# A short convolution of 464 tokens moved from TensorE to GpSimd, in a kernel of convolution and gated feed-forward layers

## The chip, the cores and the metric

The kernel runs on one core of a Trainium2 chip. The core has TensorE (PE in the profile; its weight loads are PEld), VectorE (DVE), ScalarE (ACT), GpSimd (POOL) and SyncE (SP), which here only issues DMAs. The metric is device time in microseconds; less is better. The median of three runs of the kernel before is 763.82 us (762.99 to 764.46).

## What is computed

The input `x` is 8 x 4096 x 192. Each of the 192 channels belongs to one of 8 heads of 24 channels, and each head has 7 taps, the softmax of its row of `weight`. A causal convolution along the 4096 tokens applies them, and a feed-forward layer of width 1536 with a gate follows:

```python
x_pad = np.concatenate([np.zeros((B, K - 1, D)), x], axis=1)
x_unf = x_pad[:, idx, :].reshape(B, S, K, H, group)      # idx[s, k] = s + k
x = np.einsum('hk,bskhg->bshg', softmax(weight), x_unf)  # the convolution
out = (np.maximum(x @ w_gate, 0) * (x @ w_val)) @ w_out  # the feed-forward layer
```

## The kernel before

**Units.** The 8 sequences are split into two streams of four, which lie side by side on the partitions: 64 channels of stream 0 and 64 of stream 1, in three chunks `c`. A unit is 1024 tokens of both streams, in two windows of 512. There are 16 units. `xc[u]` holds the convolved tokens of unit `u`, channels on partitions.

**Stages of a unit.** `gate_val` (L560 the matmuls, L571 the relu on ScalarE, L572 the product on VectorE) makes 24 blocks of the hidden layer, 12 for each window. The projection (`project_turn`, L582) then runs over three output tiles `p`, each in two turns, in the order (0,0) (1,0) (0,1) (2,0) (1,1) (2,1). After turn 0 of a tile ScalarE copies one column of it (`between_turns`, L595), so that turn 1, which writes the same tile, waits for ScalarE. After turn 1 VectorE transposes the tile into the output buffer (`turn_out`, L600). All PSUM tiles come from one ring of four, `ps`.

**The convolution, two ways.** Units 0 and 1 are convolved on TensorE, with the taps spread into band matrices. Unit 0 by `conv_steps`, straight into `xc[0]`. Unit 1 by `conv(2)` and `conv(3)` (L409), during the projection of unit 0: eight matmuls each, tokens on partitions, then five ScalarE copies out of PSUM (L422) and five DMA transposes into `xc[1]` (L441). `conv(2)` makes the first 560 tokens of unit 1, `conv(3)` the other 464.

Units 2 to 15 are convolved tap by tap off TensorE, by a lane that runs one to two units ahead. For unit `u`: `lane_load` loads the tokens (L250, issued by GpSimd); `lane_turn` lets GpSimd sort them (L462) and the SP queue transpose them (L464) into `x_r`, with the last 16 tokens of the unit before copied in front (L452). During the projection of unit `u-2`, `lane_first` (L510) and `product` (L490) on ScalarE multiply by taps, and `lane_rest` on VectorE runs twelve `scalar_tensor_tensor` steps (L521) and one `tensor_scalar` (L531), in portions of 6, 5 and 2, each ahead of one `turn_out`. During the gate stage of unit `u-1`, GpSimd adds the seven products of the remaining 1792 elements of each partition (`add`, L499), the last add writing `xc[u]`.

**What sets the order.** Nothing is rescheduled (`tc.manual_schedule()`): each engine and each DMA queue runs its instructions in the order in which the program writes them, and waits by semaphores. Most pools have one buffer for a name: `x_e`, `x_p` and each `prod` tile are used again by the next unit, which waits until the last reader is done.

Of the kernel before, what the change touches and what calls it, by code (L numbers as in the profile page):

```python
# [8 lines left out]
FP = mybir.dt.float32  # L9
F16 = mybir.dt.float16  # L10
ACTF = mybir.ActivationFunctionType
ALU = mybir.AluOpType
# [3 lines left out]
def kernel(  # L16
# [12 lines left out]
    nc = tc.nc  # L29

    B, S, D = x.shape
# [4 lines left out]
    NB = B // 2  # L36
# [9 lines left out]
    WARM = [(4, 4, 4, 1), (4, 4, 1)]  # L46
    STEPS0 = [1, 0, 2, 3, 4]
    CONV1 = 10


    UNIT = 2 * WIN
# [4 lines left out]
    TILES = UNIT // 128  # L56
    GROUPS = [(0, [WIN * w + SUB * j for j in range(GSUB)]) for w in range(2)]
    second = [min(t, 2 * UNIT - SUB) for t in range(UNIT, 2 * UNIT, SUB)]
    GROUPS += [(0, second[:GSUB]), (0, second[GSUB:])]

    ctx.enter_context(tc.manual_schedule())
    const = ctx.enter_context(tc.tile_pool(name="const", bufs=1))
# [13 lines left out]
    def staged(i, j):  # L76
        return stages[i][:, XH * j : XH * (j + 1)]
# [163 lines left out]
    def lane_load(u, streams=range(2)):  # L241


        bp, t0 = u * UNIT // S, u * UNIT % S
        if u not in xes:
            xes[u] = epool.tile([128, TILES, 2, NCH, 64], F16, name="x_e"), None
        xe, head = xes[u]
        for st in streams:
            row = (bp + NB * st) * S + t0
            nc.gpsimd.dma_start(  # L250
                out=xe[:, :, st, :, :].rearrange("p j c r -> p j (c r)"),
                in_=bass.AP(
                    tensor=x.tensor,
                    offset=x.offset + row * D,
                    ap=[[D, 128], [128 * D, TILES], [1, D]],
                ),
            )
        if 1 in streams and t0 and u - 1 not in xes and u - 1 not in xrs:
            head = const.tile([HALO, 2, NCH, 64], F16, name="head")
            nc.gpsimd.dma_start(  # L260
                out=head[:].rearrange("p s c r -> p s (c r)"),
                in_=bass.AP(
                    tensor=x.tensor,
                    offset=x.offset + (bp * S + t0 - HALO) * D,
                    ap=[[D, HALO], [NB * S * D, 2], [1, D]],
                ),
            )
        xes[u] = xe, head

    for s in range(4):  # L270
        load_w(s)
# [4 lines left out]
    load_x(1, range(1, 2))  # L276
    for s in (6, 7):
        pool_halves(s)
    lane_load(2, range(1))
    for s in (8, 9):  # L280
        pool_halves(s)
    lane_load(2, range(1, 2))

    mx = const.tile([128, 1], FP)
    nc.vector.tensor_reduce(
# [113 lines left out]
    def conv(g):  # L399


        xt = xts.pop(g)
        bp, toks = GROUPS[g]
        n = len(toks)
        rows = SUB + PAD
        W = 2 * n * G
        pair = [psum.tile([128, 2, 512], FP, name="ps") for _ in range(2)]
        for h, (t, bank, slot) in PLACE.items():
            nc.tensor.matmul(  # L409
                out=pair[t][0:SUB, bank, W * slot : W * (slot + 1)],  # L410
                lhsT=band(h),
                rhs=xt[0:rows, 0:n, :, G * h : G * (h + 1)],
                start=True,
                stop=True,
                skip_group_check=True,
            )
        y = staged(1, g - 1).rearrange("p (j c s r) -> p j c s r", c=NCH, s=2, r=64)
# [28 lines left out]
    def lane_turn(u):  # L446
        xe, head = xes.pop(u)
        xr = rpool.tile([128, NCH, HALO + UNIT], F16, name="x_r")
        if u * UNIT % S == 0:
            nc.gpsimd.memset(xr[:, :, 0:HALO], 0.0)  # L450
        elif head is None:
            nc.gpsimd.tensor_copy(out=xr[:, :, 0:HALO], in_=xrs[u - 1][:, :, UNIT : UNIT + HALO])  # L452
        else:
            turned = const.tile([HALO, NCH, 2, 64], F16, name="turned")
            for st in range(2):
                nc.gpsimd.tensor_copy(out=turned[:, :, st, :], in_=head[:, st, :, :])
            nc.sync.dma_start_transpose(
                out=xr[:, :, 0:HALO], in_=turned[:].rearrange("p c s r -> p (c s r)")
            )
        xp = epool.tile([128, TILES, NCH, 2, 64], F16, name="x_p")  # L460
        for st in range(2):
            nc.gpsimd.tensor_copy(out=xp[:, :, :, st, :], in_=xe[:, :, st, :, :])  # L462
        for j in range(TILES):
            nc.sync.dma_start_transpose(  # L464
                out=xr[:, :, HALO + 128 * j : HALO + 128 * j + 128],
                in_=xp[:, j].rearrange("p c s r -> p (c s r)"),
            )
        xrs[u] = xr

    def pieces(lo, hi):  # L470

# [11 lines left out]
    def flat(u):  # L483
        return xc[u][:].rearrange("p c t -> p (c t)")
# [9 lines left out]
                    scale=tap[:, c, k : k + 1],  # L494
                )

    def add(u, k):
        p0 = prods[u, 0]
        nc.gpsimd.tensor_tensor(  # L499
            out=p0[:] if k < KW - 1 else flat(u)[:, LDVE:FLAT],  # L500
            in0=p0[:],
            in1=prods.pop((u, k))[:],
            op=ALU.add,
        )
# [35 lines left out]
    def gate_val(u, w):  # L540
        h = hpool.tile([128, NFF, 2, WIN], F16, name="hT")
        xcb = xc[u]
        for f in range(NFF):
# [25 lines left out]
            for sts in [slice(0, 1), slice(1, 2)] if u == 0 and w == 0 and f == 0 else [slice(0, 2)]:  # L569
                gr = gpool.tile([128, 2, WIN], F16, name="gr")  # L570
                nc.scalar.activation(out=gr[:, sts], in_=pss[0][:, sts], func=ACTF.Relu)  # L571
                nc.vector.tensor_tensor(out=h[:, f, sts], in0=gr[:, sts], in1=pss[1][:, sts], op=ALU.mult)  # L572
        return h

    def project_turn(hs, p, ps, turn):
# [84 lines left out]
    )  # L660
    for u in range(NUNIT):
        lane = 1 <= u < NUNIT - 1
        if lane:
            add(u + 1, 1)
        if u == 1:
            lane_load(3)
            add(2, 2)
            add(2, 3)
        if u + 2 < NUNIT:
            lane_turn(u + 2)  # L670
        if u == 0:
            xts[3] = load_x(3)
            wide = plain.rearrange("k (f a p d) -> k f a p d", a=2, p=3, d=32)
            for a in range(2):
                nc.gpsimd.tensor_copy(out=Wo[:, :, :, 32 * a : 32 * a + 32], in_=wide[:, :, a, :, :])
        if lane:
            for k in range(4 if u == 1 else 2, KW - 1):
                if k == KW - 2 and 1 < u < NUNIT - 3:
                    lane_load(u + 3, range(1))
                add(u + 1, k)  # L680
            if 1 < u < NUNIT - 3:
                lane_load(u + 3, range(1, 2))
        hs = [gate_val(u, w) for w in range(2)]
        if lane:
            add(u + 1, KW - 1)
        if u == 1:
            lane_load(4)
        if u == 0:
            xc[1] = xcpool.tile([128, NCH, UNIT], F16, name="xc")
            conv(2)  # L690
        del xc[u]
        bp, w0 = u * UNIT // S, u * UNIT % S // WIN
        lane = None
# [9 lines left out]
        for p, turn in ((0, 0), (1, 0), (0, 1), (2, 0), (1, 1), (2, 1)):  # L703
            if turn == 0:
                tiles[p] = psum.tile([128, 2, 512], FP, name="ps")
            project_turn(hs, p, tiles[p], turn)
            if turn == 0:
                between_turns(tiles[p])
                if u == 0 and p == 0:
                    conv(3)  # L710
                if lane:
                    for k in TAPS[p]:
                        product(u + 2, k)
                if u == 0 and p == 1:
                    psum.tile([128, 2, 512], FP, name="ps")
                continue
            if lane:
                for _ in range(STEPS[p]):
                    next(lane)
            turn_out(tiles[p], o, p)  # L720
# [31 lines left out]
```

## Time and profile before

| | |
|---|---|
| median of 3 runs | 763.82 us |
| the profiled execution, its own time | 763.18 us |
| its span | 761.2 us |
| mean granted clock of TensorE | 0.999 |
| busy: PE / DVE / ACT / POOL | 757.1 / 669.9 / 604.0 / 425.0 us |
| start of unit 1, 2, 3 on TensorE | 58.30 / 104.97 / 151.60 us |

The span is what the profiler saw of the engines; the execution's own time has some 2 us more around it. Times on the axis of the trace count from the span's start. In a row of the timeline, the first number is the start, the second how long the instructions of the row lasted from first start to last end, and brackets at the end give the idle time of that engine before it and what ended it. In a group, the numbers behind the bar are the total busy time, the mean of one instruction in ns, and the idle time before them.

### The profile page before, as it was taken

The page shows a single profiled execution, that of the slowest core. Times are in us where ns is not written, and L with a number is a line of the kernel's source. Part 1 is how long each engine was busy: PE and PEld are TensorE (multiplying, and loading weights), DVE is VectorE, ACT ScalarE, POOL GpSimd, SP SyncE. Part 2 cuts the span into 40 slices and gives each one's busy share as a digit, 9 for nine tenths or more (in the row PEclk, how much of TensorE's full clock was granted, in tenths as well). Part 3 has the DMA queues.
Part 4 walks back from the last instruction along what each step waited for, and adds up shares of the span by engine and source line. Part 5 has one row for each costly group of instructions (what it writes and reads, how often), then busy time and mean ns, then how long its engine had stood idle before and what let it go on. Part 6 is the DMA issues. An engine that isn't in the chain of part 4 may idle for free.

```text
span 761.2 us, 30408 instructions
## 1 busy us (share of the span) xinstructions
PE 757.1 (99%) x13732; PEld 497.5 (65%) x13732; DVE 669.9 (88%) x634; ACT 604.0 (79%) x671; POOL 425.0 (56%) x200
## 2 busy tenths in 40 slices
PE   9999999999999999999999999999999999999998
PEld 5556666666666666666666666666666666666668
DVE  7879989998998989989899899998999989896691
ACT  7898887878878788787877878788797887874471
POOL 8608749094591936829277391864909558092000
PEclk9999999999999999999999999999999999999999
DMA  9927536054450534516255152442715432030302
GB/s 149 154 56 131 85 82 86 5 121 49 95 76 6 126 42 98 72 27 119 28 106 65 48 102 23 111 59 70 88 14 121 49 88 42 3 84 3 86 3 84
DMA packets 154513, 54.36 MB, mean 71 GB/s; under 512 B 149632, under 2 KB 154384, under 8 KB 154384
## 3 DMA queue, kind: packets, MB, share of 16 engines
q1 hardware_dynamic: 117600, 37.87, 22.6%
q0 software_dynamic: 36352, 14.26, 17.1%
q8 instruction: 107, 1.75, 0.9%
q10 hardware_dynamic: 432, 0.30, 0.1%
q14 instruction: 22, 0.18, 0.1%
HBM read 29.40 MB, written 25.17 MB: 72 GB/s over the span
## 4 chain that ended last, share of the span: by engine, by line
PE 99%; DMA 0%; ACT 0%; issue 0%
PE ps L560 65%; PE ps L582 31%; PE ps L625 2%; PE ps L386 0%; PE ps L409 0%; DMA w<-in_weight_dram 0%; PE ps L195 0%; PE ps L330 0%; PE ps L211 0%; PE ps L205 0%; ACT out_s L636 0%; ACT L129 0%
## 5 line engine op out<-in xcount | busy, mean ns | idle before, releaser
L572 DVE TENSOR_TENSOR hT<-gr,ps 128x1024 f16<-128x1024 f16 (+1 forms) x385 | 468.9, 1218 | 35.3 <-ACT gr L571 8.3
L571 ACT ACTIVATE gr<-ps 128x1024 f16<-128x1024 f32 (+1 forms) x385 | 392.8, 1021 | 116.5 <-PE ps L560 116.5
L499 POOL TENSOR_TENSOR prod<-prod,prod 128x1792 f32<-128x1792 f32 x70 | 279.5, 3993 | 258.6 <-DVE prod L531 230.8
L560 PE MATMUL ps<-xc,Wg 64*64 64x512 f16 (+1 forms) x4464 | 324.3, 376 | 0.0
L560 PE MATMUL ps<-xc,Wv 64*64 64x512 f16 (+1 forms) x4464 | 324.2, 376 | 0.0
L582 PE MATMUL ps<-hT,Wo 64*64 64x512 f16 x4320 | 236.3, 376 | 0.0
L560 PEld LDWEIGHTS <-Wg 64*64 64x64 f16 (+1 forms) x4464 | 163.5, 107 | 85.2
L560 PEld LDWEIGHTS <-Wv 64*64 64x64 f16 (+1 forms) x4464 | 157.0, 106 | 91.4 <-DVE hT L572 0.3
L582 PEld LDWEIGHTS <-Wo 64*64 64x64 f16 x4320 | 153.9, 107 | 78.9 <-issue 0.3
L490 ACT ACTIVATE prod<-x_r,tap 128x1024 f32<-128x1024 f16 (+1 forms) x182 | 175.1, 1044 | 0.0
L521 DVE SCALAR_TENSOR_TENSOR acc<-x_r,tap,acc 128x1024 f32<-128x1024 f16 (+1 forms) x140 | 113.2, 874 | 2.0 <-ACT acc L510 2.0
L600 DVE STREAM_TRANSPOSE out_s<-ps 128x1024 f32<-128x1024 f32 x45 | 56.1, 1247 | 33.3 <-PE ps L582 28.8
L499 POOL TENSOR_TENSOR xc<-prod,prod 128x1792 f16<-128x1792 f32 x14 | 56.0, 4001 | 0.4
L462 POOL COPY x_p<-x_e 128x1536 f16<-128x1536 f16 x28 | 40.3, 1463 | 0.1
L250 POOL DMA_DIRECT2D x_e<-in_x_dram x28 | 25.5, 911 | 0.0
L595 ACT COPY turned_by<-ps 128x2 f32<-128x2 f32 x45 | 7.0, 156 | 21.8 <-PE ps L582 19.9
L521 DVE SCALAR_TENSOR_TENSOR xc<-x_r,tap,acc 128x1024 f16<-128x1024 f16 (+1 forms) x28 | 24.1, 859 | 0.0
L510 ACT ACTIVATE acc<-x_r,tap 128x1024 f32<-128x1024 f16 (+1 forms) x28 | 21.6, 821 | 0.0
L625 PEld LDWEIGHTS <-hT 128*128 128x128 f16 x192 | 15.8, 98 | 0.4 <-issue 0.4
L625 PE MATMUL ps<-Wo,hT 128*128 128x192 f16 x192 | 16.0, 246 | 0.0
L636 ACT COPY out_s<-ps 128x768 f32<-128x768 f32 (+2 forms) x5 | 3.2, 638 | 12.7 <-PE ps L625 12.7
L636 DVE COPY out_s<-ps 128x192 f32<-128x192 f32 x1 | 0.4, 356 | 13.3 <-PE ps L625 13.3
(58 smaller groups left out, 72.4 us busy)
## 6 DMA issues: line engine op xcount, KB each, us to landing
out_dram<-out_s SPq DMA_DIRECT2D x121, 192.0 KB
x_e<-in_x_dram POOLq DMA_DIRECT2D x28, 384.0 KB, 5.3
x_r<-x_p SPq DMA_TRANSPOSE x112
out_dram<-out_s SPq DMA_DIRECT2D x3, 384.0 KB
out_s<-in_x_dram POOLq DMA_DIRECT2D x4, 240.0 KB, 6.7
prod<-in_moe_w_out_dram POOLq DMA_DIRECT2D x1, 576.0 KB, 9.1
prod<-in_x_dram SPq DMA_DIRECT2D x2, 192.0 KB
out_s<-in_x_dram POOLq DMA_DIRECT2D x2, 192.0 KB, 4.9
```

The lines of the kernel that those rows point to most:

```text
L250: nc.gpsimd.dma_start(out=xe[:, :, st, :, :].rearrange("p j c r -> p j (c r)"), in_=bass.AP(tensor=x.tensor, offset=x.offset + row * D, ap ...
L462: nc.gpsimd.tensor_copy(out=xp[:, :, :, st, :], in_=xe[:, :, st, :, :])
L490: nc.scalar.activation(out=prods[u, k][:, at - LDVE : at - LDVE + n], in_=shifted(u, c, k, t, n), func=ACTF.Copy, scale=tap[:, c, k : k + 1],)
L499: nc.gpsimd.tensor_tensor(out=p0[:] if k < KW - 1 else flat(u)[:, LDVE:FLAT], in0=p0[:], in1=prods.pop((u, k))[:], op=ALU.add,)
L510: nc.scalar.activation(out=accs[u][:, at : at + n], in_=shifted(u, c, 0, t, n), func=ACTF.Copy, scale=tap[:, c, 0:1],)
L521: nc.vector.scalar_tensor_tensor(out=(flat(u) if k == KW - 1 else acc)[:, at : at + n], in0=shifted(u, c, k, t, n), scalar=tap[:, c, k : k ...
L560: nc.tensor.matmul(out=pss[i][q : q + M, st, :], lhsT=W[64 * st : 64 * st + 64, c, 128 * f + q : 128 * f + q + M], rhs=xcb[64 * st : 64 * ...
L571: nc.scalar.activation(out=gr[:, sts], in_=pss[0][:, sts], func=ACTF.Relu)
L572: nc.vector.tensor_tensor(out=h[:, f, sts], in0=gr[:, sts], in1=pss[1][:, sts], op=ALU.mult)
L582: nc.tensor.matmul(out=ps[64 * st : 64 * st + 64, b, :], lhsT=Wo[64 * r : 64 * r + 64, f, p, :], rhs=hs[b][64 * r : 64 * r + 64, f, st, :] ...
L600: nc.vector.transpose(out=o[:].rearrange("p t (b d) -> p b t d", b=2)[:, :, :, 32 * p : 32 * p + 32], in_=ps[:].rearrange("p b (t c) -> p ...
L625: nc.tensor.matmul(out=ps[:, i // 2, D * (i % 2) : D * (i % 2) + D], lhsT=h[:, f, st, 128 * q : 128 * (q + 1)], rhs=Wo[:, f, :, :].rearran ...
```

## The change

`conv(3)` is taken out: its loads, its eight matmuls, its copies and transposes, and a spare PSUM tile allocated beside it. The 464 tokens of unit 1 are convolved tap by tap instead.

- `rest_load` loads the last 512 tokens of unit 1, one DMA for each stream, ahead of the loads of unit 2. `rest_turn` sorts them on GpSimd (two copies of 768 elements) and transposes them (four DMA transposes on SP's queue, in front of the eight of unit 2) into `x_r1`. The 16 tokens in front of unit 2 are now copied from `x_r1`, and the small load `head` and its transpose go.
- `rest_pool`: GpSimd multiplies 3 x 464 elements by taps 0 to 4, the tap broadcast along the tokens, and sums them: five multiplies and four adds. They stand in its queue during unit 0, behind `lane_turn(2)` and the copies of `Wo`. The first product goes into `out_s` space (`rest["sum"]`), the others into a tile of the name `x_p` (`rest["new"]`), which unit 2's transposes read before.
- `rest_scalar`: ScalarE makes the product of tap 6 for two chunks, behind the eighth and the twelfth relu of the second window of unit 0. `rest_vector`: VectorE makes four products, tap 5 for three chunks and tap 6 for one, between the gate stage and the projection of unit 0.
- `rest_end`: at the head of unit 1's instructions GpSimd adds tap 5 (one add of 1392 elements) and tap 6 (three adds of 464), which write the last 464 columns of `xc[1]`.
- In unit 1, GpSimd's order is now: `rest_end`, `lane_load(3)`, adds of unit 2 for taps 6 and 5, `lane_turn(3)`, adds for taps 4, 3, 2, 1, `lane_load(4)`. Before it was: one add, `lane_load(3)`, two adds, `lane_turn(3)`, three adds, `lane_load(4)`. Later units keep their order.

```diff
-    GROUPS += [(0, second[:GSUB]), (0, second[GSUB:])]
+    GROUPS += [(0, second[:GSUB])]
+    REST = SUB * GSUB - WIN
+    NREST = WIN - REST
...
+    xr1 = const.tile([128, NCH, WIN], F16, name="x_r1")
+    def rest_turn():
+        for st in range(2):
+            nc.gpsimd.tensor_copy(out=xp1[:, :, :, st, :], in_=xe1[:, :, st, :, :])
+        for j in range(WIN // 128):
+            nc.sync.dma_start_transpose(
+                out=xr1[:, :, 128 * j : 128 * j + 128],
+                in_=xp1[:, j].rearrange("p c s r -> p (c s r)"),
+            )
...
-    lane_load(2, range(1))
+    rest_load(0)
     for s in (8, 9):
         pool_halves(s)
-    lane_load(2, range(1, 2))
+    rest_load(1)
+    lane_load(2)
...
+    def rest_at(k, cs=slice(0, NCH)):
+        o = REST - KW + 1 + k
+        return xr1[:, cs, o : o + NREST]
...
+    def rest_pool():
+        for k in range(KW - 2):
+            nc.gpsimd.tensor_tensor(
+                out=rest["new" if k else "sum"],
+                in0=rest_at(k),
+                in1=tap[:, :, k : k + 1].to_broadcast([128, NCH, NREST]),
+                op=ALU.mult,
+            )
+            if k:
+                nc.gpsimd.tensor_tensor(
+                    out=rest["sum"], in0=rest["sum"], in1=rest["new"], op=ALU.add
+                )
...
+    def rest_end():
+        nc.gpsimd.tensor_tensor(out=rest["sum"], in0=rest["sum"], in1=rest[KW - 2], op=ALU.add)
+        for c in range(NCH):
+            nc.gpsimd.tensor_tensor(
+                out=xc[1][:, c, WIN + REST : UNIT],
+                in0=rest["sum"][:, c, :],
+                in1=rest[KW - 1][:, c, :],
+                op=ALU.add,
+            )
...
+            if u == 0 and w == 1 and f in RESTF:
+                rest_scalar(RESTF.index(f))
...
         if u == 0:
-            xts[3] = load_x(3)
+            rest_turn()
+            lane_turn(2)
             wide = plain.rearrange("k (f a p d) -> k f a p d", a=2, p=3, d=32)
             for a in range(2):
                 nc.gpsimd.tensor_copy(out=Wo[:, :, :, 32 * a : 32 * a + 32], in_=wide[:, :, a, :, :])
+            rest_parts()
+            rest_pool()
+        elif u == 1:
+            rest_end()
+            lane_load(3)
+            for k in range(KW - 1, 0, -1):
+                if k == KW - 3:
+                    lane_turn(3)
+                add(2, k, 1)
+            lane_load(4)
...
             conv(2)
+            for k, c in [(KW - 2, c) for c in range(NCH)] + [(KW - 1, NCH - 1)]:
+                rest_vector(k, c)
...
-                if u == 0 and p == 0:
-                    conv(3)
...
-                if u == 0 and p == 1:
-                    psum.tile([128, 2, 512], FP, name="ps")
```

More of the change, by code (lines that the diff above doesn't have):

```diff
@@ L48 @@
     CONV1 = 10
+    RESTF = [7, 11]
     UNIT = 2 * WIN
@@ L245, in lane_load @@
         if u not in xes:
-            xes[u] = epool.tile([128, TILES, 2, NCH, 64], F16, name="x_e"), None
-        xe, head = xes[u]
+            xes[u] = epool.tile([128, TILES, 2, NCH, 64], F16, name="x_e")
+        xe = xes[u]
         for st in streams:
@@ L257, in lane_load, with rest_load @@
             )
[L258 to L266, printed above, removed]
+    xe1 = stages[1][:, 0 : WIN // 128 * 2 * D].rearrange("p (j s c r) -> p j s c r", s=2, c=NCH, r=64)
+    xp1 = stages[1][:, XH : XH + WIN // 128 * 2 * D].rearrange(
+        "p (j c s r) -> p j c s r", c=NCH, s=2, r=64
+    )
+    xr1 = const.tile([128, NCH, WIN], F16, name="x_r1")
+    def rest_load(st):
+        nc.gpsimd.dma_start(
+            out=xe1[:, :, st, :, :].rearrange("p j c r -> p j (c r)"),
+            in_=bass.AP(
+                tensor=x.tensor,
+                offset=x.offset + (NB * st * S + UNIT + WIN) * D,
+                ap=[[D, 128], [128 * D, WIN // 128], [1, D]],
+            ),
+        )
[6 more added lines that the diff above has]
+                in_=xp1[:, j].rearrange("p c s r -> p (c s r)"),
             )
-        xes[u] = xe, head
     for s in range(4):
@@ L416, in conv @@
             )
-        y = staged(1, g - 1).rearrange("p (j c s r) -> p j c s r", c=NCH, s=2, r=64)
+        y = staged(1, 0).rearrange("p (j c s r) -> p j c s r", c=NCH, s=2, r=64)
         def move(copy, t, bank, i0, step_in, c, r0, step_out, width):
@@ L446, in lane_turn @@
     def lane_turn(u):
-        xe, head = xes.pop(u)
+        xe = xes.pop(u)
         xr = rpool.tile([128, NCH, HALO + UNIT], F16, name="x_r")
@@ L450, in lane_turn @@
             nc.gpsimd.memset(xr[:, :, 0:HALO], 0.0)
-        elif head is None:
+        elif u > 2:
             nc.gpsimd.tensor_copy(out=xr[:, :, 0:HALO], in_=xrs[u - 1][:, :, UNIT : UNIT + HALO])
[L453 to L459, printed above, removed]
         xp = epool.tile([128, TILES, NCH, 2, 64], F16, name="x_p")
@@ L467, in lane_turn, with rest_parts, rest_scalar, rest_vector @@
             )
+        if u == 2:
+            nc.gpsimd.tensor_copy(out=xr[:, :, 0:HALO], in_=xr1[:, :, WIN - HALO : WIN])
         xrs[u] = xr
+    def rest_at(k, cs=slice(0, NCH)):
+        o = REST - KW + 1 + k
+        return xr1[:, cs, o : o + NREST]
+    rest = {}
+    def rest_parts():
+        rest["sum"] = stages[1][:].bitcast(FP)[:, XH // 2 : XH // 2 + NCH * NREST]
+        held_e = epool.tile([128, TILES, 2, NCH, 64], F16, name="x_e")
+        rest[KW - 1] = held_e[:].rearrange("p j s c r -> p (j s c r)").bitcast(FP)[:, 0 : NCH * NREST]
+        held_p = epool.tile([128, TILES, NCH, 2, 64], F16, name="x_p")
+        rest["new"] = held_p[:].rearrange("p j c s r -> p (j c s r)").bitcast(FP)[:, 0 : NCH * NREST]
+        rest[KW - 2] = xc[0][:].rearrange("p c t -> p (c t)").bitcast(FP)[:, 0 : NCH * NREST]
+        for k in list(rest):
+            rest[k] = rest[k].rearrange("p (c t) -> p c t", t=NREST)
+    def rest_pool():
[10 more added lines that the diff above has]
+                )
+    def rest_scalar(c):
+        nc.scalar.activation(
+            out=rest[KW - 1][:, c, :],
+            in_=rest_at(KW - 1, c),
+            func=ACTF.Copy,
+            scale=tap[:, c, KW - 1 : KW],
+        )
+    def rest_vector(k, c):
+        nc.vector.tensor_scalar(
+            out=rest[k][:, c, :],
+            in0=rest_at(k, c),
+            scalar1=tap[:, c, k : k + 1],
+            scalar2=None,
+            op0=ALU.mult,
+        )
+    def rest_end():
[6 more added lines that the diff above has]
+                op=ALU.add,
+            )
     def pieces(lo, hi):
@@ L495, in product, with add @@
                 )
-    def add(u, k):
+    def add(u, k, last=KW - 1):
         p0 = prods[u, 0]
         nc.gpsimd.tensor_tensor(
-            out=p0[:] if k < KW - 1 else flat(u)[:, LDVE:FLAT],
+            out=p0[:] if k != last else flat(u)[:, LDVE:FLAT],
             in0=p0[:],
@@ L662 @@
         lane = 1 <= u < NUNIT - 1
[L663 to L670, printed above, removed]
         if u == 0:
-            xts[3] = load_x(3)
+            rest_turn()
+            lane_turn(2)
             wide = plain.rearrange("k (f a p d) -> k f a p d", a=2, p=3, d=32)
@@ L675 @@
                 nc.gpsimd.tensor_copy(out=Wo[:, :, :, 32 * a : 32 * a + 32], in_=wide[:, :, a, :, :])
-        if lane:
-            for k in range(4 if u == 1 else 2, KW - 1):
-                if k == KW - 2 and 1 < u < NUNIT - 3:
+            rest_parts()
[8 more added lines that the diff above has]
+            lane_load(4)
+        elif lane:
+            add(u + 1, 1)
+            if u + 2 < NUNIT:
+                lane_turn(u + 2)
+            for k in range(2, KW - 1):
+                if k == KW - 2 and u < NUNIT - 3:
                     lane_load(u + 3, range(1))
                 add(u + 1, k)
-            if 1 < u < NUNIT - 3:
+            if u < NUNIT - 3:
                 lane_load(u + 3, range(1, 2))
         hs = [gate_val(u, w) for w in range(2)]
-        if lane:
+        if lane and u > 1:
             add(u + 1, KW - 1)
-        if u == 1:
-            lane_load(4)
         if u == 0:
```

## The prediction

> **What bounds the kernel now.** I read the page's busy times first, then its chain of waits, then that chain in order of time, to see what the removed piece occupies.
>
> ```profile
> PE 757.1 (99%) x13732; PEld 497.5 (65%) x13732; DVE 669.9 (88%) x634; ACT 604.0 (79%) x671; POOL 425.0 (56%) x200
> PE 99%; DMA 0%; ACT 0%; issue 0%
> ...
> 40.56 0.99 PE ps L409 x8
> 41.55 2.71 PE ps L582 x48
> 44.27 0.96 PE ps L409 x8
> 45.22 13.07 PE ps L582 x240
> 58.30 31.13 PE ps L560 x576
> 89.43 15.54 PE ps L582 x288
> ```
>
> TensorE is the whole chain: whatever it no longer does is saved, and whatever it must wait for is lost, for no later stage has slack to give it back (every unit is 31.1 + 15.54 us of TensorE). The second row of L409 is the piece that goes: 0.96 us. GpSimd is busy 56%, so it looks free; where, its timeline and the table of windows tell (the windows are two projections, a gate stage, a projection).
>
> ```profile
> 31.76 2.23 POOL L675 COPY Wo<-prod 128x1152 f16<-128x1152 f16 x2
> 59.26 4.00 POOL L499 TENSOR_TENSOR prod<-prod,prod 128x1792 f32<-128x1792 f32 x1 [25.27 <-ACT prod L490]
> 63.20 1.81 POOL L250 DMA_DIRECT2D x_e<-in_x_dram  x2
> 65.02 8.08 POOL L499 TENSOR_TENSOR prod<-prod,prod 128x1792 f32<-128x1792 f32 x2
> 73.04 0.24 POOL L452 COPY x_r<-x_r 128x48 f16<-128x48 f16 x1
> 73.19 3.04 POOL L462 COPY x_p<-x_e 128x1536 f16<-128x1536 f16 x2
> ...
> 41.50:58.10 16.60, 16.60 (x297) 9.14 (x300) 13.05 (x16) 16.38 (x28) 0.00 (x0) 1.00 0.24 54
> 89.40:105.00 15.60, 15.60 (x296) 10.42 (x289) 14.07 (x17) 14.51 (x19) 0.65 (x1) 1.00 0.46 53
> 105.00:136.00 31.00, 31.00 (x580) 20.29 (x576) 28.90 (x24) 24.07 (x24) 28.53 (x11) 1.00 0.63 105
> 136.00:151.60 15.60, 15.60 (x296) 10.42 (x290) 14.08 (x17) 14.53 (x19) 0.00 (x0) 1.00 0.01 2
> ```
>
> The hole is 34.0 to 59.3. But the windows (columns PE, PEld, DVE, ACT, POOL) show that GpSimd computes only in gate stages and never in a projection, while VectorE runs its L521 steps (`scalar_tensor_tensor`, two tensors from SBUF) only in projections. No row shows the two side by side. Last, the queue of DMA transposes, ScalarE and VectorE, because the new work hangs on them:
>
> ```profile
> 29.23 11.17 SPq L464 DMA_TRANSPOSE x_r<-x_p  x8
> 76.26 11.61 SPq L464 DMA_TRANSPOSE x_r<-x_p  x8
> ...
> 89.75 1.54 ACT L510 ACTIVATE acc<-x_r,tap 128x1024 f32<-128x1024 f16 x2
> 92.07 0.16 ACT L595 COPY turned_by<-ps 128x2 f32<-128x2 f32 x1 [0.79 <-PE ps L582]
> ...
> 44.22 4.86 DVE L521 SCALAR_TENSOR_TENSOR acc<-x_r,tap,acc 128x1024 f32<-128x1024 f16 x6 [2.00 <-ACT acc L510]
> ```
>
> Eight transposes take 11.2 to 12.3 us. Those of unit 3 end at 87.87 and L510, which reads them, starts at 89.75: under 2 us to spare. Behind L510 in ScalarE's order stands L595, and turn 1 of a projection tile writes over what L595 reads, so TensorE waits for it.
>
> **Removed from TensorE.** `conv(3)`: 0.96 us in the chain. The whole projection of unit 0 is 2.71 + 0.96 + 13.07 = 16.74 against 15.54 in later units, so 0.96 to 1.20; I take 1.1. Its five ScalarE copies (2.00) and five transposes go too, off the path. Unit 1 would start at 58.3 - 1.1 = 57.2. That is the most the change can gain: 0.15%. About 0.2% (1.5 us) is what a measurement of this kernel can tell from no change.
>
> **ScalarE and VectorE products.** Two ScalarE products of 464: L510 takes 1.19 for 1024 and 0.49 for 256, so about 0.7 each. The first stands between two relus that leave 0.27 idle each, so some 0.4 is pushed on; VectorE, at 1.22 of every 1.295, can't recover it; TensorE loses up to 0.4, I take 0.3. The second delays L510 of unit 2, covered by VectorE's 1.55 us idle before its first L600. Four VectorE products (768 elements take 0.61, so some 0.45 each, 1.8 together) fit the 2.00 idle before L521. Path: +0.3.
>
> **When GpSimd can start.** The issues of `load_x(3)` (2.6) and `head` (0.5) go, two loads of 0.76 come; the loads of unit 2 are issued some 3 us later, still before GpSimd needs them at 26. On SP's queue four new transposes stand in front of unit 2's eight: 26.4 + 12 x 1.31 + 0.8 (one of the early ones took 2.05) = 42.9, and the last one lands 1.1 later, as before's did: 44.0. `conv(2)`'s five transposes behind them end near 50, in time for 57. The first multiply needs only the four new ones, but the second writes into the x_p tile that the eight still read (`rest["new"]`). So it starts at 44.0, not in the hole.
>
> **How long.** GpSimd has no two-input row but L499: 1792 elements in 3.99, 4.04 from start to start. Its copies take 0.50 for 384 and 1.46 for 1536, so 0.18 fixed; then 1392 elements are 3.14 and 464 are 1.17. A multiply by a broadcast tap is in no row: between a one-input copy (1392: 1.34) and an add (3.14); I take the add, as both read two operands. From 44.0 there are 4 multiplies, 5 adds and 3 short adds: 9 x 3.14 + 3 x 1.17 = 31.8. `rest_end` ends at 75.8 if nothing disturbs it; TensorE wants its last channel at 57.2 + 15.5 + 0.4 = 73.2, so it stalls 2.6.
>
> **What is moved behind it.** Load, adds and turn of unit 3 come after `rest_end`: load 1.8, two adds 8.1, halo and copies 3.2: 88.9 (before: 76.2). Transposes 11.6 and landing 1.1: 101.6, L510 and L595 1.7: 103.3. TensorE wants turn 1 of the first tile two runs of 2.59 after its projection starts (57.2 + 31.1 + 2.6 = 90.9), at 96.1: 7.2 lost. VectorE's L521 steps start 10 us late (102.6 against 92.5); 1.4 of that is its idle time before L600 and 7.2 is TensorE's own wait, so unit 2's first product is about 1.3 late. Together 2.6 + 7.2 + 1.3 = 11.1 without any interference. Adds of unit 2 end near 105, before unit 2 starts; later units keep their order.
>
> **Interference, the unknown term.** From 44.0 GpSimd's steps lie beside VectorE's twelve L521 steps. The price lies between nothing and full turn-taking. GpSimd takes 2.13 ns an element for two inputs and 0.83 for one, so its adds are bound by reading; rows beside L572 (one tensor from SBUF, one from PSUM) show 3.99 to 4.04, no price, but that is not the form here. I take turn-taking: eleven pairs, GpSimd 9 x 3.14 + 2 x 1.17 = 30.6 and VectorE 4.86 + 3.23 + 1.28 = 9.4, then the last transposes and steps as in the row from 102.83 to 106.34, 3.5. VectorE's first product of unit 1 starts at 44.0 + 43.5 = 87.5 instead of 60.1 - 1.1 + 0.3 = 59.3, and TensorE, which needs the PSUM tiles that VectorE empties, loses 28.2 less the 0.3 it can run ahead. The stalls of the last two paragraphs then vanish, for `rest_end` ends near 85 and unit 1's second half starts only near 101, its projection near 116, after unit 3's transposes (about 110).
>
> The Trainium skill (SBUF — State Buffer, Who interferes with whom) says that a VectorE instruction with two SBUF inputs and a GpSimd instruction that reads SBUF shut each other out for a whole instruction. No row here shows it. By that rule the sum is this one, without it the first rival's.
>
> **Sum.** -1.1 + 0.3 + 27.9 = +27.1 on the profiled execution's 763.18 (span 761.2 and 1.98 around it) is 790.3; the median of the runs is 0.64 above that execution, so 790.9. Pairs are not always both ready, so I say 790.
>
> **Rivals.**
> 1. No interference: GpSimd and VectorE run side by side. For: every add in the page costs the same, whatever VectorE does. Against: never beside L521. +11.1 - 0.8 = 774.1. With multiplies at 2.2 us `rest_end` is 3.8 earlier, the 2.6 goes and the 7.2 is 6.0: 770.
> 2. They exclude each other, but VectorE keeps going while its next step is ready, so GpSimd gets in only between VectorE's runs. First run held 2.9, the later ones by one GpSimd step each: unit 1's first product 5.7 late; `rest_end` ends at 86, 7.0 after it is wanted; then the 7.2 and 1.3 as above and 1 for adds beside L521: 22.2 - 0.8 = 785.2. If GpSimd keeps going instead, VectorE's steps wait for all of it: 44.0 + 31.8 + 9.4 + 1.2 + 3.5 = 89.9 for the first product, 30.6 late, 793.
> 3. Not slower: multiplies at copy speed, no interference and transposes done by 41.5. Then `rest_end` ends at 41.5 + 4 x 1.34 + 5 x 3.14 + 3.5 = 66.1, unit 3's transposes land at 91.9, and L595 is done at 93.6, just when TensorE wants it. It decides at that 66: each us later costs one. Time 763.0. Against: no two-input row near copy speed, and all three must hold.
>
> **Chances.** Forecast 0.43; rival 1 0.27; rival 2 0.18, its variant 0.07; rival 3 0.05, which by its gain of 0.8 is mostly within 0.2%. The range runs from rival 1 with cheaper multiplies (770) to the variant (794); the forecast's own is 786 to 793. Slower 0.95, same 0.03, faster 0.02.
>
> **What would show it.** Right: L521 steps after 44 start 3 us apart, each at the end of a GpSimd step; VectorE's first L572 of unit 1 near 87; a hole of over 20 us in TensorE at the start of unit 1. Rival 1: L521 keeps 1.27, a hole of 2 to 3 us at the middle of unit 1, and one of 7 us before its third projection run, ended by L595. The step on the second multiply is wrong if it starts before 42. The whole is wrong if `rest_end` ends before 67.

## The result: 789.5 us, and the profile after

The changed kernel takes 789.48 us (median of 6 runs, 788.72 to 791.26), the kernel before, run on the same chip, 763.63 (762.85 to 764.46). The ratio is 1.0343, 95% interval 1.0328 to 1.0358: slower by 26 us. The profiled execution took 790.11, its span is 788.4, 27.2 more than before. In the changed kernel the familiar lines have new numbers: gate and value matmuls L633, relu L644, product L645, projection L657, VectorE's convolution steps L594, its transposes of output tiles L675, `between_turns` L670, GpSimd's adds for later units L572. The new work is L505 (multiplies), L512 (adds), L517 (ScalarE's products), L525 (VectorE's products), L534 and L536 (`rest_end`).

First the page, its busy times and its chain, and under it pieces of that chain in order of time (start, duration, what):

```profile
PE 761.6 (97%) x13724; PEld 498.5 (63%) x13724; DVE 695.2 (88%) x638; ACT 603.3 (77%) x668; POOL 459.3 (58%) x211
PEclk9996799999999999999999999999999999999999
PE 89%; DVE 4%; DMA 3%; POOL 2%; issue 1%; SPq 0%; ACT 0%; DVEq 0%; ACTq 0%; POOLq 0%
```

```profile
30.69 7.95 DMA x_r<-out_s
39.33 1.01 ACT gr L644
...
47.79 6.00 DVE xc L525 x2
53.80 3.29 DVE x_e L525
57.08 13.51 DVE acc L594 x5
...
85.56 30.90 PE ps L633 x519
116.46 15.54 PE ps L657 x277
132.00 31.09 PE ps L633 x571
```

TensorE was the whole chain before; now a stretch of the chain ahead of 85.56 is a DMA, then VectorE. From there on a unit again takes 30.9 and 15.54. Unit 1's projection begins at 116.46 (before: 89.43) and unit 2 at 132.00 (104.97): both 27.03 later. So all of the loss is made before unit 1's gate stage is under way, and none is given back. What TensorE waited for (total, times, longest), and GpSimd's and VectorE's timelines in that stretch:

```profile
PE ps L633 <- DVE out_s L675: 20.2, 3, 14.7
PE ps L633 <- ACT gr L644: 2.2, 1, 2.2
```

```profile
41.05 2.51 POOL L505 TENSOR_TENSOR out_s<-x_r,tap 128x1392 f32<-128x1392 f16 x1
45.11 2.51 POOL L505 TENSOR_TENSOR x_p<-x_r,tap 128x1392 f32<-128x1392 f16 x1 [1.55 <-DMA x_r<-x_p]
47.69 3.21 POOL L512 TENSOR_TENSOR out_s<-out_s,x_p 128x1392 f32<-128x1392 f32 x1
...
56.90 2.55 POOL L505 TENSOR_TENSOR x_p<-x_r,tap 128x1392 f32<-128x1392 f16 x1
59.53 4.01 POOL L512 TENSOR_TENSOR out_s<-out_s,x_p 128x1392 f32<-128x1392 f32 x1
...
73.58 4.45 POOL L536 TENSOR_TENSOR xc<-out_s,x_e 128x464 f16<-128x464 f32 x3
```

```profile
46.62 7.18 DVE L525 TENSOR_SCALAR xc<-x_r,tap 128x464 f32<-128x464 f16 x3
53.72 3.37 DVE L525 TENSOR_SCALAR x_e<-x_r,tap 128x464 f32<-128x464 f16 x1
57.01 3.53 DVE L594 SCALAR_TENSOR_TENSOR acc<-x_r,tap,acc 128x1024 f32<-128x1024 f16 x1
...
57.01 18.88 DVE L594 SCALAR_TENSOR_TENSOR acc<-x_r,tap,acc 128x1024 f32<-128x1024 f16 x6
75.80 1.24 DVE L675 STREAM_TRANSPOSE out_s<-ps 128x1024 f32<-128x1024 f32 x1
76.97 4.13 DVE L594 SCALAR_TENSOR_TENSOR acc<-x_r,tap,acc 128x1024 f32<-128x1024 f16 x4
81.02 1.27 DVE L594 SCALAR_TENSOR_TENSOR xc<-x_r,tap,acc 128x1024 f16<-128x1024 f16 x1
...
85.44 1.18 DVE L645 TENSOR_TENSOR hT<-gr,ps 128x1024 f16<-128x1024 f16 x1
```

Six L594 steps take 18.88 us where the same six took 4.86. Read the first of them (the row with x1, from a narrower window) against GpSimd: it starts at 57.01, GpSimd's multiply runs from 56.90 to 59.45, and the step ends at 60.54, 1.09 after that; GpSimd's add starts at 59.53 and ends at 63.54, 3.00 after the step has ended. Each waits inside its own duration, for the whole of the other's instruction. Such a wait shows as a long instruction and not as idle time: the busy share of VectorE is 88% as before, and only its sum has grown by 25.3 us. The four new L525 products are 10.5 of the growth, and L594's group is 15.0 of it (before: 113.2 in all, 874 ns for one):

```profile
L594 DVE SCALAR_TENSOR_TENSOR acc<-x_r,tap,acc 128x1024 f32<-128x1024 f16 (+1 forms) x140 | 128.2, 982 | 0.0
```

The L594 steps that start after GpSimd's last add (78.03) are as short as before. Unit 1's first product is at 85.44 instead of 60.12, 25.3 later. The other 1.7 of the 27.0 is TensorE's clock. The table of windows (length, then PE, PEld, DVE, ACT, POOL; then the granted clock, DMA share and GB/s) shows it:

```profile
62.00:78.00 16.00, 1.28 (x20) 0.61 (x13) 16.00 (x7) 1.02 (x1) 15.69 (x7) 0.59 0.00 0
...
85.00:88.00 3.00, 2.44 (x25) 1.33 (x27) 2.44 (x3) 1.02 (x1) 3.00 (x1) 0.50 0.48 115
88.00:91.00 3.00, 3.00 (x52) 1.82 (x48) 1.62 (x2) 2.05 (x2) 2.92 (x2) 0.87 0.92 224
91.00:94.00 3.00, 3.00 (x60) 1.89 (x56) 2.83 (x3) 2.19 (x3) 3.00 (x3) 1.00 0.81 189
```

The runs of matmuls behind the last of TensorE's waits, in order of time:

```profile
85.56 1.50 PE L633 MATMUL ps<-xc,Wv 64*64 64x512 f16 x12 [0.56 <-DVE out_s L675]
86.80 1.54 PE L633 MATMUL ps<-xc,Wg 64*64 64x512 f16 x12
88.08 1.19 PE L633 MATMUL ps<-xc,Wv 64*64 64x512 f16 x12
89.08 0.84 PE L633 MATMUL ps<-xc,Wg 64*64 64x512 f16 x12
```

After this hole the granted clock is half, and a run of 12 matmuls comes 1.24 to 1.28 us after the one before it instead of 0.65, until about 89 us.

### The profile page after: what moved, and what is told of

Read it like the earlier page. It is cut to its first block, busy times and chain, and to the rows that moved or that the text cites. A ratio compares the mean times of both kernels' runs of the same rounds, so it can differ in the third digit from the quotient of the medians.

```text
span 788.4 us, 30418 instructions
## 1 busy us (share of the span) xinstructions
PE 761.6 (97%) x13724; PEld 498.5 (63%) x13724; DVE 695.2 (88%) x638; ACT 603.3 (77%) x668; POOL 459.3 (58%) x211
## 4 chain that ended last, share of the span: by engine, by line
PE 89%; DVE 4%; DMA 3%; POOL 2%; issue 1%; SPq 0%; ACT 0%; DVEq 0%; ACTq 0%; POOLq 0%
PE ps L633 59%; PE ps L657 28%; DVE acc L594 2%; PE ps L700 2%; DMA x_r<-out_s 1%; DMA x_e<-in_x_dram 1%; DVE xc L525 1%; DMA Wv<-in_moe_w_val_dram 1%; DVE out_s L675 0%; DVE x_e L525 0%; POOL Wv L236 0%; POOL Wg L236 0%; SPq L284 0%; POOL Wg L229 0%; ACT gr L644 0%
## 5 line engine op out<-in xcount | busy, mean ns | idle before, releaser
L645 DVE TENSOR_TENSOR hT<-gr,ps 128x1024 f16<-128x1024 f16 (+1 forms) x385 | 468.9, 1219 | 40.4 <-ACT gr L644 12.8
L644 ACT ACTIVATE gr<-ps 128x1024 f16<-128x1024 f32 (+1 forms) x385 | 392.7, 1021 | 141.7 <-PE ps L633 141.7
L572 POOL TENSOR_TENSOR prod<-prod,prod 128x1792 f32<-128x1792 f32 x70 | 279.2, 3989 | 241.5 <-DVE prod L604 221.0
L633 PE MATMUL ps<-xc,Wv 64*64 64x512 f16 (+1 forms) x4464 | 326.8, 378 | 15.6 <-DVE out_s L675 15.3
L633 PE MATMUL ps<-xc,Wg 64*64 64x512 f16 (+1 forms) x4464 | 326.5, 378 | 7.1 <-DVE out_s L675 4.9
L657 PE MATMUL ps<-hT,Wo 64*64 64x512 f16 x4320 | 236.1, 376 | 0.0
L633 PEld LDWEIGHTS <-Wv 64*64 64x64 f16 (+1 forms) x4464 | 157.8, 106 | 109.3 <-issue 19.2
L633 PEld LDWEIGHTS <-Wg 64*64 64x64 f16 (+1 forms) x4464 | 164.1, 107 | 93.8 <-issue 9.7
L657 PEld LDWEIGHTS <-Wo 64*64 64x64 f16 x4320 | 153.9, 107 | 79.0 <-issue 0.2
L594 DVE SCALAR_TENSOR_TENSOR acc<-x_r,tap,acc 128x1024 f32<-128x1024 f16 (+1 forms) x140 | 128.2, 982 | 0.0
L675 DVE STREAM_TRANSPOSE out_s<-ps 128x1024 f32<-128x1024 f32 x45 | 56.1, 1247 | 31.9 <-PE ps L657 29.2
L572 POOL TENSOR_TENSOR xc<-prod,prod 128x1792 f16<-128x1792 f32 x14 | 56.0, 4001 | 0.4
L594 DVE SCALAR_TENSOR_TENSOR xc<-x_r,tap,acc 128x1024 f16<-128x1024 f16 (+1 forms) x28 | 24.1, 862 | 0.0
L670 ACT COPY turned_by<-ps 128x2 f32<-128x2 f32 x45 | 7.0, 156 | 21.7 <-PE ps L657 19.9
L512 POOL TENSOR_TENSOR out_s<-out_s,x_p 128x1392 f32<-128x1392 f32 x4 | 14.4, 3601 | 0.3
## 6 DMA issues: line engine op xcount, KB each, us to landing
prod<-in_moe_w_out_dram POOLq DMA_DIRECT2D x1, 576.0 KB, 15.3
```

The costliest lines, as they stand in the source:

```text
L572: nc.gpsimd.tensor_tensor(out=p0[:] if k != last else flat(u)[:, LDVE:FLAT], in0=p0[:], in1=prods.pop((u, k))[:], op=ALU.add,)
L594: nc.vector.scalar_tensor_tensor(out=(flat(u) if k == KW - 1 else acc)[:, at : at + n], in0=shifted(u, c, k, t, n), scalar=tap[:, c, k : k ...
L633: nc.tensor.matmul(out=pss[i][q : q + M, st, :], lhsT=W[64 * st : 64 * st + 64, c, 128 * f + q : 128 * f + q + M], rhs=xcb[64 * st : 64 * ...
L657: nc.tensor.matmul(out=ps[64 * st : 64 * st + 64, b, :], lhsT=Wo[64 * r : 64 * r + 64, f, p, :], rhs=hs[b][64 * r : 64 * r + 64, f, st, :] ...
L675: nc.vector.transpose(out=o[:].rearrange("p t (b d) -> p b t d", b=2)[:, :, :, 32 * p : 32 * p + 32], in_=ps[:].rearrange("p b (t c) -> p ...
```

## The experiments

The theory is that of the prediction: GpSimd's steps and VectorE's L594 (L521 before) shut each other out and take turns. Its rivals are that they don't interfere (the time goes elsewhere: late data, long products, GpSimd simply too slow), and that they slow each other in some other proportion.

**Nine adds in the kernel before.** Nothing else is changed; the adds stand where `rest_pool` would.

```diff
+            spare = const.tile([128, 1024], FP, name="spare")
+            nc.gpsimd.memset(spare[:], 0.0)
+            for _ in range(9):
+                nc.gpsimd.tensor_tensor(out=spare[:], in0=spare[:], in1=spare[:], op=ALU.add)
```

> The kernel before, with nine adds of 1024 elements (both operands in SBUF, 2.36 us each by the slope of the copies and adds of before) put into GpSimd's queue behind the copies of Wo, on a scratch tile that nobody reads. They would lie from 34.9 to 56.7. Theory (GpSimd's steps and VectorE's steps with two SBUF operands take turns): the adds beside L572, up to 42, keep 2.4 us and slow nothing; from 44.2 five adds each hold up one L521 step by 2.36, the first step waits 0.4, and VectorE has 1.55 idle to spare: 0.4 + 11.8 - 1.55 = 10.6, so 774.2. Rival 1 (no interference; the changed kernel's VectorE steps are long for a reason of their own): 763.6, L521 at 1.27. Rival 2 (GpSimd only gets in when VectorE pauses): L521 starts at most 2.4 late, under 766, and the adds spread until 63.

769.82 us (769.43 to 770.83), ratio 1.0082 (1.0066 to 1.0097). VectorE's and GpSimd's timelines:

```profile
44.04 11.64 DVE L521 SCALAR_TENSOR_TENSOR acc<-x_r,tap,acc 128x1024 f32<-128x1024 f16 x6 [2.00 <-ACT acc L510]
...
56.78 3.23 DVE L521 SCALAR_TENSOR_TENSOR acc<-x_r,tap,acc 128x1024 f32<-128x1024 f16 x4
```

```profile
34.70 19.50 POOL L679 TENSOR_TENSOR spare<-spare 128x1024 f32<-128x1024 f32 x9
```

No data are shared, no engine waits by a semaphore for the adds, and yet the six steps take 11.64 instead of 4.86; after the last add they are as fast as before. With nothing but the adds put in, that is interference. The size was missed: these adds took 1.89 each and not the 2.36 of the estimate, so fewer of them lay beside L521. TensorE waited 3.6; the other 3.1 of the 6.7 by which the span grew are runs at half clock.

**Six adds.** The same with `range(6)`.

> The same with six adds, which would end at 49.4. Theory: 0.4 + 2 x 2.36 - 1.55 = 3.6, so 767.2; the difference to nine adds is 3 x 2.36 = 7.1. Rival 1: 763.6. Rival 2: under 766, and the same as with nine.

763.68 us (763.49 to 764.02), ratio 0.9999 (0.9990 to 1.0009). The six steps took 6.55:

```profile
44.70 6.55 DVE L521 SCALAR_TENSOR_TENSOR acc<-x_r,tap,acc 128x1024 f32<-128x1024 f16 x6 [2.00 <-ACT acc L510]
```

The 1.7 more fell into the 1.55 us that VectorE idles ahead of its first transpose. This transpose starts at 51.17 instead of 50.64, but the steps had started 0.48 later in this execution already. The expectation missed for the same reason as above. Here turn-taking cost nothing, since it stayed about within the slack behind it.

**Copies, and writes alone.** In place of the adds, `for _ in range(20): nc.gpsimd.tensor_copy(out=spare[:], in_=spare[:])`, and `for _ in range(24): nc.gpsimd.memset(spare[:], 0.0)`.

> The same with twenty in-place copies of 1024 float32 elements instead of the adds (one operand read, 1.03 us each by the slope of before's float16 copies), which would lie from 34.9 to 56.5. Theory, if any GpSimd step that reads SBUF takes its turn: some eleven copies each hold up one VectorE step: 11 x 1.03 - 1.55 = 9.8, so 773.4. Rival (only GpSimd steps with two operands collide): 763.6, L521 at 1.27.

> The same with twenty-four memsets of 1024 float32 elements (GpSimd only writes; at some 0.8 us each they would lie from 35 to 55). Theory, if it is the reading that is shared: 763.6, L521 at 1.27. Rival (any GpSimd instruction that moves data shuts VectorE's two-operand steps out): some ten memsets hold up one step each, 10 x 0.8 - 1.55 = 6.5, so 770.

The copies: 771.31 us (770.48 to 771.76), ratio 1.0098 (1.0083 to 1.0113), the six steps 8.97 and the next four 6.31 (before 3.23):

```profile
45.28 8.97 DVE L521 SCALAR_TENSOR_TENSOR acc<-x_r,tap,acc 128x1024 f32<-128x1024 f16 x6 [2.00 <-ACT acc L510]
```

The writes: 763.63 (763.46 to 765.35), ratio 1.0004 (0.9994 to 1.0013), the six steps as before:

```profile
44.49 4.87 DVE L521 SCALAR_TENSOR_TENSOR acc<-x_r,tap,acc 128x1024 f32<-128x1024 f16 x6 [2.00 <-ACT acc L510]
...
57.95 0.86 DVE L531 TENSOR_SCALAR prod<-x_r,tap 128x768 f32<-128x768 f16 x1
```

So it is GpSimd's reading of SBUF that L521 collides with, one operand being enough. The second row adds something: VectorE's `tensor_scalar`, one tensor in and one out, took 0.86 beside the memsets (0.61 without), and the memset that starts at 58.46, beside it, took 1.25 instead of 0.95. This one pair says that it collides with writes also.

**The change without GpSimd's chain** (taps 1 to 4 and the add of tap 5). This kernel leaves five of the seven taps out for the last 464 tokens of unit 1.

```diff
-        for k in range(KW - 2):
+        for k in range(1):
...
-        nc.gpsimd.tensor_tensor(out=rest["sum"], in0=rest["sum"], in1=rest[KW - 2], op=ALU.add)
```

> The changed kernel without GpSimd's taps 1 to 5 (four multiplies and five adds left out; tap 0, tap 6 and all products of ScalarE and VectorE stay, so the last 464 tokens of unit 1 lack five taps). Theory: what GpSimd's chain costs by taking turns goes, the late product of ScalarE stays. Unit 0's projection starts 4.5 late as in the changed kernel, 1.1 is saved by the convolution taken off TensorE, and the three short adds beside L594 cost up to 2: 767 to 769, L594 at 1.27. Rival (VectorE's steps are long for another reason, such as their place or operands): near 789.

765.78 us (764.19 to 766.44), ratio 1.0028 (1.0016 to 1.0039). Some 23.7 us of the loss hang on the chain. L593 (the same step) is back at 5.44 for six and 3.23 for four:

```profile
48.73 5.44 DVE L593 SCALAR_TENSOR_TENSOR acc<-x_r,tap,acc 128x1024 f32<-128x1024 f16 x6 [0.47 <-ACT acc L582]
```

What is left is a wait of 1.7 for a relu at the end of unit 0, with half clock behind it:

```profile
PE ps L632 <- ACT gr L643: 1.7, 1, 1.7
```

**ScalarE's first product three relus later.**

```diff
-    RESTF = [7, 11]
+    RESTF = [10, 11]
```

> The changed kernel with ScalarE's first product behind the eleventh relu instead of the eighth, when the four new transposes have landed. Unit 0's projection then starts at 41.8 to 42.3 instead of 45.99. Theory (turn-taking is what ends last): GpSimd's second multiply still waits for the transposes until 45.1, VectorE's four products get done before it, and the same nine GpSimd steps now each hold up one L594 step: only some 2 are saved, 787. Rival (the late product is a cost of its own that adds to the rest): 789.5 - 4 = 785.5 or less.

788.21 us (787.58 to 788.33), ratio 1.0321 (1.0306 to 1.0337). Unit 0's projection starts at 41.45 instead of 45.99, so the wait for the relu is gone. Of these 4.5 us only 1.8 reach the end (span 786.6), because VectorE comes to its steps earlier and meets more of GpSimd's chain there: L525 takes 1.89 for three and is mostly clear of it, but the six L594 start at 46.60 and take 19.22, and TensorE waits 22.0 for L675.

```profile
46.60 19.22 DVE L594 SCALAR_TENSOR_TENSOR acc<-x_r,tap,acc 128x1024 f32<-128x1024 f16 x6 [2.04 <-ACT acc L583]
```

**Both.**

> Both: without GpSimd's taps 1 to 5, and ScalarE's first product behind the eleventh relu. Theory: all that is left is the 1.1 saved on TensorE, 0.3 to 0.7 for the products, and up to 2 for three short adds beside L594: 763 to 765. It bounds what the change could have gained. Rival (something else of the change costs, such as the later loads or the order of unit 1's adds): over 766.

764.07 us (763.40 to 765.18), ratio 1.0006 (0.9997 to 1.0016). Even without the chain the removed 0.96 us brings nothing: unit 0's projection starts 0.5 later than before (42.01), and there are waits of 0.7 for L674 and 0.3 for L669.

**The same work, moved beside unit 1's gate stage**, where VectorE's L645 reads one tensor from SBUF and one from PSUM.

```diff
-            rest_pool()
         elif u == 1:
+            add(2, KW - 1, 1)
+            rest_pool()
             rest_end()
             lane_load(3)
-            for k in range(KW - 1, 0, -1):
+            for k in range(KW - 2, 0, -1):
```

> The changed kernel with GpSimd's whole chain behind its first add of unit 2, which waits for VectorE's last lane step of unit 0's projection, so that no GpSimd step lies beside L594. Theory: L594 is back at 1.27 and unit 1 starts near 61.6; but the chain (5 multiplies of 2.5, 5 adds of 3.2, 3 short adds, after one add of 4.0) ends near 98 while TensorE wants it at 77: a wait of 20 on GpSimd at the middle of unit 1, and some 3 for unit 3's later transposes: 763.5 + 3.4 + 20 + 3 = 790. Rival (no turn-taking): the same chain, but then the changed kernel itself would not have had its long VectorE steps; L594 would be 3 us here too.

792.24 us (791.27 to 793.21), ratio 1.0376 (1.0355 to 1.0396). L594 is 4.87 again, and the groups (in all, mean ns of one) show two of the colliding steps undisturbed; in the change the means were 3601 and 2445:

```profile
L512 POOL TENSOR_TENSOR out_s<-out_s,x_p 128x1392 f32<-128x1392 f32 x4 | 12.5, 3123 | 0.3
```

```profile
L525 DVE TENSOR_SCALAR xc<-x_r,tap 128x464 f32<-128x464 f16 x3 | 1.2, 456 | 0.0
```

```profile
PE ps L633 <- POOL xc L536: 19.6, 3, 18.6
```

The interference is gone and the time is no better: GpSimd then starts at 65.75, is done at 97.98, and TensorE waits 19.6 for `rest_end` itself. Between VectorE's last lane step of unit 0 (it ends at 61.65) and the use of the sums, near 77, there is no place for 32 us of GpSimd.

**Shorter GpSimd steps, same work.** Each step of 1392 elements is cut into three of 464. If the two share by time, nothing changes; if they take turns one instruction for one, VectorE waits less for each of its own.

```diff
-            nc.gpsimd.tensor_tensor(
-                out=rest["new" if k else "sum"],
-                in0=rest_at(k),
-                in1=tap[:, :, k : k + 1].to_broadcast([128, NCH, NREST]),
-                op=ALU.mult,
-            )
+            for c in range(NCH):
+                nc.gpsimd.tensor_tensor(
+                    out=rest["new" if k else "sum"][:, c, :],
+                    in0=rest_at(k, c),
+                    in1=tap[:, c, k : k + 1].to_broadcast([128, NREST]),
+                    op=ALU.mult,
+                )
...
```

> The changed kernel with each of GpSimd's multiplies and adds of 1392 elements cut into three of 464, the same work in 27 + 3 steps of about 0.96 (multiply) and 1.17 (add). Theory (one whole GpSimd step per VectorE step): VectorE's 16 steps between 46.6 and its last transpose now wait for one short step each, some 16 x 1.05 = 17 instead of nine long ones with 26; its first product of unit 1 comes near 78 instead of 85.4, and GpSimd's chain ends near 86, before TensorE's second half of unit 1 at 92: 789.5 - 7.3 = 782. Rival (the two share by time, not by instruction): the same total work takes as long, or a little longer for the fixed part of more steps: 789 to 792.

783.30 us (782.60 to 785.15), ratio 1.0251 (1.0234 to 1.0268). It is turns, one for one: six steps take 9.59 instead of 18.88. Step by step, the first (48.57) ends at 50.40, 1.08 after GpSimd's multiply of 48.36; the next multiply (49.28) then takes 1.94 instead of 0.95 and ends at 51.22, and the second step ends at 51.50, behind it. The lines are L598 (convolution steps), L649 (product), L679 (transposes), L674 (`between_turns`):

```profile
48.57 9.59 DVE L598 SCALAR_TENSOR_TENSOR acc<-x_r,tap,acc 128x1024 f32<-128x1024 f16 x6 [2.86 <-ACT acc L587]
...
72.12 1.18 DVE L649 TENSOR_TENSOR hT<-gr,ps 128x1024 f16<-128x1024 f16 x1
```

```profile
PE ps L637 <- DVE out_s L679: 10.4, 3, 7.9
PE ps L661 <- ACT turned_by L674: 5.7, 2, 5.5
```

The first product of unit 1 is 13.3 us earlier than in the change, the span only 5.0. Not all of the 13.3 is due to shorter turns: in this execution unit 0's projection starts at 43.45 instead of 45.99, and VectorE's four products end at 45.72, before GpSimd's second multiply starts (47.44), so that they wait for nothing. GpSimd, which now gives way more often, ends `rest_end` at 86.07 instead of 78.03, while TensorE wants it sooner; what stands behind it is late, unit 3's transposes land at 112.3, L587 (first products of unit 3) waits 8.56 for them, and L674 behind it holds TensorE for 5.5. That is the second wait of the prediction's rival 1.

**Unit 3's turn earlier.** The kernel of the last run, with the turn copies after one add of unit 1 instead of two.

```diff
-                if k == KW - 3:
+                if k == KW - 2:
                     lane_turn(3)
```

> The kernel of 'split' (each 1392-element GpSimd step cut into three of 464 elements, 783.3 us), with the turn copies of unit 3 placed after the first ordinary GpSimd tap of unit 1 instead of after the second. Theory: the 5.5 us that TensorE waits in 'split' for the turned copies at the second-last projections come from unit 3's transposes, which land at 112.5; the turn copies come some 4 us earlier, the transposes start and land about 4 us earlier, that wait shrinks by about 4, and the time is about 779.5 us. Rival: the wait is not due to the transposes (GpSimd's taps are late for unit 2 whatever the turn does), or the copies merely push the tap that they pass: 783 us or more.

785.08 us (784.26 to 786.63), ratio 1.0283 (1.0266 to 1.0301). The named wait did go: none for L674 in this stretch. But the time did not fall: the two profiled executions are level (785.18, and 785.15 for the run before), for two reasons that the trace shows. That the median is 1.8 above that run's is not explained by these traces. VectorE now starts unit 3's L598 steps at 108.14, while GpSimd still adds for unit 2 (to 114.88), and the old pair takes turns too: 10.20 for six instead of 6.23, and TensorE waits 2.9 for L679:

```profile
108.14 10.20 DVE L598 SCALAR_TENSOR_TENSOR acc<-x_r,tap,acc 128x1024 f32<-128x1024 f16 x6
```

From the start of unit 1's projection to that of unit 2 it is 51.8 us instead of 54.7. These 2.9 are offset in the profiled execution by a later start of unit 0's projection (46.72 against 43.45), where the data for ScalarE's first product landed later. The halo copy that needs the same data (L482) starts between 37.49 and 39.13 in the runs that keep this order; why it moves is open, and this edit comes after it.

## Why the prediction was right

It said 790.0, and 789.5 was measured, by the mechanism that it took for likeliest. Its terms were less exact than their sum: 4.2 too little for the products and 4.3 too much for turn-taking cancel. That the sum is met to 0.1 us is luck.

| term | predicted | measured (profiled executions) |
|---|---|---|
| `conv(3)` removed | -1.1 | -1.08: unit 0's projection 15.57 instead of 16.65 |
| ScalarE's and VectorE's products | +0.3 | +4.5: unit 0's projection starts at 45.99 instead of 41.48 |
| turn-taking | +27.9 | +23.6: 20.2 of waits for L675, 3.4 at half clock |
| sum | +27.1 | +27.0 |

- **The step that failed: ScalarE's product.** Its duration was right (0.68, for 0.7). What was left out is its wait. It needs `x_r1`, whose four transposes were issued from 26.7 to 31.9; the one of 30.69 landed at 38.6, 7.95 us after its issue (the chain's first row). The next relus stand behind the product, TensorE waits 2.2 and 0.4, and some 2.0 more goes at half clock. The prediction took landing at 1.1. In this stretch the DMA share is 1.50 and 1.59 (30 to 38 us) instead of 1.23 and 0.83 before, and `Wo` now lands 15.3 us after its issue instead of 9.1. That the loads delay the transposes fits this, but no run took the loads away. The 4.5 is not a cost that adds to the rest in full: with the wait gone (ScalarE's first product three relus later) only 1.8 of it came off the span.
- **VectorE's four products.** Sized right (0.46 in the run with the chain moved), placed wrong: they were to fit 2.00 of idle time, and took 10.5 us, since they take turns as well: the four end at 47.87, 51.16, 53.80 and 57.09, each 0.3 after the end of a GpSimd step. The prediction limited the collision to steps with two SBUF inputs. The Trainium skill (SBUF — State Buffer, Who interferes with whom) says also that `tensor_scalar` can enter a mode that uses both of VectorE's port pairs and then contends with GpSimd. The trace agrees that it contends: 0.46 alone, 2.4 beside GpSimd, and 0.86 for 0.61 beside GpSimd's writes; which mode the engine was in is in no row.
- **Eleven pairs.** They were four products and some seven steps; L594 came to the chain only at 57.01, and its last steps ran alone after 78.03. The multiplies are 2.5 and not 3.14, the adds 3.2 to 4.0. `rest_end` ended at 78.03 (forecast near 85), the first product came at 85.44 (87.5), unit 1's projection at 116.46 (near 116). The second multiply began at 45.11 (44.0), waiting for the transposes as the prediction had it, and unit 3's transposes were in time.
- **Half clock.** No term had it. In the change it is some 2.0 at the end of unit 0 and 3.4 in unit 1 (what is left of the delay when the waits are taken off). It made up for most of what the turns cost less, which is part of the luck.

That GpSimd and VectorE exclude each other is shown by the adds alone; that it decides the time here by the run without the chain (-23.7 us); that they alternate by the cut steps. Rival 1 would have had L594 at 1.27 and 774; rival 2 the first product 5.7 late or, in its variant, 30.6 late, against 25.3 (the forecast's own was 28.2); both forms are excluded by the steps that end between GpSimd's. Rival 3 needed all of three conditions, of which none held.

No version tried beats the kernel before: the change with neither the chain nor the early product, which leaves five taps out, is only level with it.

## What to carry to other kernels

An engine's idle share doesn't say that work put there is free: look at which instructions of the other engine will lie beside it, and whether the two hold each other up. Where two engines take turns, cost each pair as the sum of both durations, and expect the waits inside the instructions, not between them. And cost a hole in TensorE with the slow matmuls that follow it.

## What the runs showed of the hardware

- GpSimd's in-place copies and two-operand adds hold up VectorE's `scalar_tensor_tensor` and are held up by it, one instruction for one: a copy takes 1.04 alone and 1.92 when it must wait. Its memsets don't. VectorE's transpose out of PSUM (L675) kept 1.24 beside it.
- GpSimd multiplies 1392 fp16 elements by a broadcast tap in 2.51 us, and adds as many in fp32 in 3.12; an in-place add of 1024 took 1.89, less than the 2.36 that the row for 1792 suggested.
- Two waits of TensorE, of 1.7 and 0.4 us with 0.8 us of matmuls between them, were enough for half clock behind them: in the run without the chain, runs of six matmuls came about 1.25 apart instead of 0.65 from 41.26 to 45. With waits of 0.9 and 0.4 at the same place (the shorter GpSimd steps) they stayed 0.65 apart. The Trainium skill (TensorE: Matmul & The Clock Gate, Part 1: The HAM clock gate) gives half rate after an idle window of about 3.4 us and full rate after as much sustained work. The ratio and roughly the recovery agree with the rows here (3.7 us of slow matmuls from 41.26 to 45); the gap that sufficed was shorter.
